# Handing score banks to the last output products in the order in which they fall free

## The chip, the cores and the metric

The kernel runs on one core of a Trainium2 chip. The metric is the device time of one execution in microseconds (us). A profile adds the span from the first to the last instruction, about 2 us shorter than that time. Engines: TensorE (matmuls; the profile calls it PE, and PEld for the loading of weights), ScalarE (ACT), VectorE (DVE), GpSimd (POOL) and SyncE (SP), which issues the stores here. L879 means line 879 of the kernel.

## The reference, cut to what matters

```python
# x: 1 x 2048 x 640;  32 heads of 20
xn = layernorm(x)
q, k, v = split(xn @ wqkv)
p = softmax(q @ k.T / sqrt(20))               # 32 x 2048 x 2048 probabilities
s = merge_heads(p @ v) @ wo                   # the "output product"
g = silu(mixer_mlp(layernorm(xn)))
return x + s * g
```

The 134 million exponentials of the softmax are the bulk. The last four blocks of 128 tokens (12 to 15) can only be finished once the last head group of their queries is done, so they form the tail of the program.

## The kernel before

The program is written by a list scheduler on the host. Every piece of work is a task; for each engine the scheduler keeps an assumed time, takes the work that is ready first by its own cost constants, and among what is ready the lowest priority number. The result is one fixed sequence of instructions for each engine, with semaphore waits where data or a PSUM bank demands one. The assumed costs decide the order only.

```python
def dv(n, rate=1.04):                 # assumed VectorE cost, ns
    return 75.0 + n * rate
...
def pe_full(fn, reads, writes, name, n):          # a full-width matmul of n columns
    t0 = max(pr.T["pe"], pr.ready("pe", reads, writes))
    c = max(pr.gate.stream(t0, n), 58.0) + pe_switch("full")    # n / 2.4 + 3 ns when warm
    pr.pe(fn, reads=reads, writes=writes, name=name, cost=c)
```

PSUM has eight banks. Bank 6 collects the attention product, banks 0 to 3 take scores for ScalarE in pairs, 4 and 5 scores for VectorE, and 7 serves all other products one at a time. When no scores are left, the score banks fall free and can hold parts of the last output products. An output product of a block is 640 columns wide: a wide part of 512 and a narrow part of 128. Each part is five "open" matmuls (L879), which need only earlier head groups, and one "closing" matmul (L884) with the last group's values in `stage_sb`.

```python
BA, BB = (5, 7), (4, 0)               # banks of blocks 14 and 15: wide, narrow
...
for i, b in enumerate(LBS):           # LBS = [14, 15]
    rq = oTall[NTB - 1] + ("wo", f"a2_{b}")
    add_job(f"tpa{i}", ...op_mms(b, ps(BA[i]), 0, 512, ..., True, False)..., rq + (f"bankoff{BA[i]}",), 60.0 + i)
    add_job(f"tpb{i}", ...op_mms(b, ps(BB[i], 128), 512, 128, ..., True, False)..., rq + (f"bankoff{BB[i]}",), 60.0 + i)
    add_job(f"tfin{i}", ...tail_fin(i)..., (f"tpa{i}", f"tpb{i}", "epL1", ...), 10.0 + i)
...
if nxt[0] >= NU:                      # no scores left to issue
    for b in act_banks:               # 0, 1, 2, 3
        if b not in bank_off and not any(b in x[1] for x in pexp):
            bank_off.add(b)
            done.add(f"bankoff{b}")
    if not bankq and 7 not in busybanks and 7 not in bank_off:
        bank_off.add(7)
        done.add("bankoff7")
```

Blocks 12 and 13 use bank 7 for their wide parts one after the other, then for both narrow parts together, which VectorE reads at L907. Only after that is bank 7 free for block 15.

Of the kernel before, what the change touches and what calls it, by code (L numbers as in the profile page):

```python
# [7 lines left out]
ALU = mybir.AluOpType  # L8
AF = mybir.ActivationFunctionType
# [273 lines left out]
class _Kern:  # L283
# [118 lines left out]
    def schedule(self):  # L402
# [22 lines left out]
        def S_(name):  # L425
            s = sl.get(name)
            if s is None:
                s = sl[name] = _Slot(name)
            return s

        bank_slot = [S_(f"bank{i}") for i in range(8)]
# [3 lines left out]
        def ps(b, n=512, off=0):  # L435
            return ps_all[:, b * 512 + off:b * 512 + off + n]

        done = set()
# [3 lines left out]
        def dv(n, rate=1.04):  # L442
            return 75.0 + n * rate

        def ac(n):
            return 90.0 + n * 0.833 + 60.0
# [340 lines left out]
        def ztmp(i, n=1):  # L787
            return zt_sb[:, 0, i % 4:i % 4 + n, :].rearrange("p a b -> p (a b)")
# [83 lines left out]
        def op_mms(b, ap, c0, n, bslot, first=True, last=True):  # L872

            steps = []
            tail = b // 4 == NTB - 1
            if first:
                for c in range(5):
                    k = 48 if c == 4 and tail else 128
                    steps.append(("pe", lambda e, c=c, k=k: e.matmul(  # L879
                        ap, oT_sb[0:k, c, b * 128:(b + 1) * 128], wo_sb[0:k, c, c0:c0 + n], start=(c == 0),  # L880
                        stop=(c == 4 and not tail)), [S_(f"oT{c}_{b // 4}"), S_("wo")], [bslot],
                        f"op{b}" if c < 4 or tail else f"opl{b}", n))
            if last and tail:
                steps.append(("pe", lambda e: e.matmul(  # L884
                    ap, stage_sb[:, (b % 4) * 128:(b % 4 + 1) * 128], wo7_sb[:, c0:c0 + n], start=False, stop=True),
                    [S_(f"stageL{last_part[b % 4]}"), S_("wo7")], [bslot], f"opl{b}", n))
            return steps
# [51 lines left out]
        def add_job(name, make, requires=(), prio=50.0):  # L939
            jobs.append(_Job(name, make if callable(make) else (lambda bk, m=make: m), requires, False, prio))  # L940
# [366 lines left out]
        for gi, (b0, nb) in enumerate(self.LN_GROUPS):  # L1307
            add_job(f"stat{gi}", stat_steps(gi), () if gi == 0 else (f"ln_s{gi - 1}",), 20.8 + b0 / 4)
            rq = (f"ln_s{gi}",) + (() if b0 < 12 else tuple(f"xT0_{d}" for d in XT[0]))
# [56 lines left out]
        for G in range(1, NG):  # L1366
            c0, c1 = 80 * (G - 1), 80 * G - 1
            for w in (1, 0):
                rq = tuple(f"qkc{w}_{j}_{tb}" for j in range(c0 // 112, c1 // 112 + 1) for tb in range(NTB)) + ("qpad",)
# [7 lines left out]
        for j in range(FC):  # L1377
            rq = hreq + xtall + ("bias", f"w1_{j // 2}")
            if j >= 4:
                rq = rq + (f"a1_{j - 4}",)  # L1380
# [10 lines left out]
        for j in range(NB):  # L1391
            rq = m1all + (f"w2_{j // 2}",) + ((f"a2_{j - 4}",) if j >= 4 else ())
# [34 lines left out]
        for p in range(NTB - 1):  # L1427
            for b in range(4 * p, 4 * p + 4):
                rq = oTall[p] + ("wo", f"ep{pidx[NG - 1, p]}", f"a2_{b}")
# [19 lines left out]
        for i, (q0, nq) in enumerate(self.QSPLIT[:-1]):  # L1449
            b0, nb = NB - 4 + q0 // 128, nq // 128  # L1450
            rq = oTall[NTB - 1] + ("wo", f"epL{i}") + tuple(f"a2_{b}" for b in range(b0, b0 + nb))
# [3 lines left out]
            add_bank_job(f"opn{b0}", opn_steps(b0, nb), rq, 30.0, NU - UP)  # L1455
            add_job(f"stl{b0}", storel_steps(b0, nb), tuple(f"res{b}" for b in range(b0, b0 + nb)), 30.0)

        BA, BB = (5, 7), (4, 0)

        def tail_fin(i):  # L1460
            b = LBS[i]
            steps = op_mms(b, ps(BA[i]), 0, 512, bank_slot[BA[i]], False, True)
            steps += op_mms(b, ps(BB[i], 128), 512, 128, bank_slot[BB[i]], False, True)
            z = ztmp(i)
            g = regC[:, b, :]
            steps.append(("act", lambda e: e.activation(z[:, 512:640], ps(BB[i], 128), AF.Copy), [bank_slot[BB[i]]],
                          [S_(f"z{i}_1")], f"tz{b}b", ac(128)))
            if i == 0:
                steps.append(("dve", lambda e: e.tensor_tensor(g[:, 0:512], ps(BA[i]), g[:, 0:512], ALU.mult),
                              [bank_slot[BA[i]], S_(f"g{b}")], [S_(f"r{b}_0")], f"tp{b}a", dv(512)))  # L1470
                steps.append(("dve", lambda e: e.tensor_tensor(g[:, 512:640], z[:, 512:640], g[:, 512:640], ALU.mult),
                              [S_(f"z{i}_1"), S_(f"g{b}")], [S_(f"r{b}_1")], f"tp{b}b", dv(128, .52)))
            else:
                steps.append(("act", lambda e: e.activation(z[:, 0:512], ps(BA[i]), AF.Copy), [bank_slot[BA[i]]],
                              [S_(f"z{i}_0")], f"tz{b}a", ac(512)))
                steps.append(("dve", lambda e: e.tensor_tensor(g, z, g, ALU.mult), [S_(f"z{i}_0"), S_(f"z{i}_1"), S_(f"g{b}")],
                              [S_(f"r{b}_0"), S_(f"r{b}_1")], f"tp{b}", dv(640, .52)))
            steps.append(("dve", lambda e: e.tensor_tensor(g, g, regA[:, b, :], ALU.add),
                          [S_(f"r{b}_0"), S_(f"r{b}_1"), S_(f"x2_{NTB - 1}")], [S_(f"res{b}")], f"tr{b}", dv(640, .52)))
            steps.append(("dma", lambda e: e.dma_start(out[0, b * 128:(b + 1) * 128, :], g), [S_(f"res{b}")], [],  # L1480
                          f"outl{b}", 163840))
            return steps

        for i, b in enumerate(LBS):
            rq = oTall[NTB - 1] + ("wo", f"a2_{b}")
            add_job(f"tpa{i}", (lambda bk, i=i, b=b: op_mms(b, ps(BA[i]), 0, 512, bank_slot[BA[i]], True, False) + [
                ("tag", f"tpa{i}")]), rq + (f"bankoff{BA[i]}",), 60.0 + i)
            add_job(f"tpb{i}", (lambda bk, i=i, b=b: op_mms(b, ps(BB[i], 128), 512, 128, bank_slot[BB[i]], True, False) + [
                ("tag", f"tpb{i}")]), rq + (f"bankoff{BB[i]}",), 60.0 + i)
            add_job(f"tfin{i}", (lambda bk, i=i: tail_fin(i)),  # L1490
                    (f"tpa{i}", f"tpb{i}", f"epL{len(self.QSPLIT) - 1}", f"x2_{NTB - 1}"), 10.0 + i)


        act_banks = [b for g in self.ACT_GROUPS for b in g]
        dve_banks = [b for g in self.DVE_GROUPS for b in g]
# [5 lines left out]
        def withdraw(bs):  # L1501
            for b in bs:
                retired.add(b)
                if b in freebanks:
                    freebanks.remove(b)
# [203 lines left out]
        bank_off = set()  # L1709
        guard = 0  # L1710
        while True:
            guard += 1
            assert guard < 400000

            if ramp[0] and "v0_15" in done:
                ramp[0] = False
                withdraw(dve_banks)
                dveready[0] = True
            if nxt[0] >= NU:
                for b in act_banks:  # L1720
                    if b not in bank_off and not any(b in x[1] for x in pexp):
                        bank_off.add(b)
                        done.add(f"bankoff{b}")
                if not bankq and 7 not in busybanks and 7 not in bank_off:
                    bank_off.add(7)
                    done.add("bankoff7")
            for dg in self.DVE_GROUPS:
                if dgrp_state[dg] == "free" and nxt[0] + self.LAST_GUARD >= NU and dveready[0] \
                        and not any(ch[0][3] == dg for ch in dchains):
                    for b in dg:  # L1730
                        if b not in bank_off:
                            bank_off.add(b)
                            done.add(f"bankoff{b}")
            activate()
            best = None
            waiting = {}
            order = sorted(("pe", "act", "dve", "pool"), key=lambda e: pr.T[e])
            acted = False
            horizon = None
            cs_by = {}  # L1740
            for e in order:
                cs = pe_cands(pr.T[e]) if e == "pe" else eng_cands(e, pr.T[e])
                cs_by[e] = cs

            bt = None
            for e in order:
                if not cs_by[e]:
                    continue
                r = min(max(x[1], pr.T[e]) for x in cs_by[e])
                if bt is None or r < bt[0]:  # L1750
                    bt = (r, e)
            if bt is None:
                break
            r, e = bt
            if e == "dve" and nxt[0] >= NU:

                soon = [max(x[1], pr.T[e]) for x in cs_by[e] if x[0] <= 12.0]
                if soon and min(soon) <= r + 130.0:
                    r = min(soon)
            ok = [x for x in cs_by[e] if x[1] <= r + 1e-6]  # L1760
            ok.sort(key=lambda x: (x[0], x[1]))
            if pr.T[e] < r:
                pr.T[e] = r
            ok[0][2]()
# [40 lines left out]
```

## Time and profile before

866.93 us, median of 3 runs (866.84 to 868.54).

| | before |
|---|---|
| span | 865.0 us |
| ScalarE busy | 845.4 us, 98% |
| VectorE busy | 823.6 us, 95% |
| TensorE busy | 797.6 us, 92% |
| last exponential ends | 855.38 us |
| tail after it | 9.6 us |

The timeline of TensorE shows its order in the tail; the columns are start, length, engine, line, operation, output and inputs, size and count, with merged rows for runs of equal instructions.

```profile
857.67 0.87 PE L879 MATMUL ps_all<-wo_sb,xnT_sb 128*128 128x128 bf16 x7
858.47 0.45 PE L884 MATMUL ps_all<-wo_sb,stage_sb 128*128 128x512 bf16 x2
858.97 1.13 PE L879 MATMUL ps_all<-wo_sb,xnT_sb 128*128 128x512 bf16 x4
860.03 0.45 PE L884 MATMUL ps_all<-wo_sb,stage_sb 128*128 128x512 bf16 x2
```

Seven narrow open matmuls (two of block 14, five of block 15), the closing pair of block 14, the wide open ones of block 15 (four of five have a record), the closing pair of block 15. A merged row shows the shape of its first instruction only.

### The profile page before, as it was taken

What the parts mean: (1) busy time and instruction counts of PE and PEld (TensorE: products, weight loads), DVE (VectorE), ACT (ScalarE), POOL (GpSimd) and SP (SyncE); (2) the same over time, 40 slices, a digit from 0 to 9 for tenths busy, and PEclk for the clock granted to TensorE, in tenths of its full rate; (3) what the DMA queues carried; (4) which work ended last, traced back from release to release, by engine and by line L of the source; (5) the groups of instructions that cost most, each with busy time, mean ns of one, the idle gap of its engine ahead of it and who ended that gap; (6) DMA issues with size and microseconds to landing.
All of it is one profiled execution on the core that took longest, in us unless ns stands there. A gap on an engine that the chain in (4) does not pass through costs nothing.

```text
span 865.0 us, 16498 instructions
## 1 busy us (share of the span) xinstructions
PE 797.6 (92%) x5828; PEld 256.1 (30%) x5918; DVE 823.6 (95%) x2047; ACT 845.4 (98%) x925; POOL 14.0 (2%) x23
## 2 busy tenths in 40 slices
PE   8899999999999999999999999999899998998997
PEld 5422222222222223222322222222222222232233
DVE  8989999999999999999999999999999999999996
ACT  7899999999999999999999999999999999999996
POOL 3200000000000000000000000000000000000000
PEclk9999999999999999999999999999999999999999
DMA  8141010011010323010013022123312201042111
GB/s 236 48 113 30 9 35 10 16 36 31 11 55 14 77 36 88 11 55 10 16 25 78 23 51 52 25 52 71 67 30 46 47 11 11 3 102 69 41 39 41
DMA packets 123350, 39.32 MB, mean 45 GB/s; under 512 B 84312, under 2 KB 122152, under 8 KB 123272
## 3 DMA queue, kind: packets, MB, share of 16 engines
q1 hardware_dynamic: 123272, 38.27, 19.4%
q8 instruction: 50, 0.82, 0.4%
q14 instruction: 28, 0.23, 0.1%
HBM read 25.88 MB, written 9.83 MB: 41 GB/s over the span
## 4 chain that ended last, share of the span: by engine, by line
ACT 87%; PE 9%; DVE 2%; POOL 1%; issue 1%; ACTq 0%; POOLq 0%
ACT pt_sb L1137 85%; PE ps_all L1109 3%; PE ps_all L1224 1%; ACT zt_sb L843 1%; PE ps_all L755 1%; PE ps_all L879 1%; ACT zt_sb L838 1%; PE ps_all L1704 1%; DVE ew_sb L1177 0%; PE ps_all L683 0%; PE ps_all L722 0%; POOL v_sb L1298 0%; PE ps_all L703 0%; DVE dpt_sb L1183 0%; PE ps_all L658 0%
## 5 line engine op out<-in xcount | busy, mean ns | idle before, releaser
L1137 ACT ACTIVATE pt_sb<-ps_all 128x1024 bf16<-128x1024 f32 x888 | 819.9, 1147 | 3.6 <-PE ps_all L1109 3.0
L1109 PE MATMUL ps_all<-qk_sb 32*128 32x512 bf16 (+1 forms) x2112 | 367.8, 377 | 48.3 <-ACT pt_sb L1137 36.7
L1177 DVE TENSOR_SCALAR ew_sb<-ps_all 128x512 uint16<-128x512 uint16 x272 | 184.2, 684 | 20.7 <-PE ps_all L1109 19.6
L1109 PEld LDWEIGHTS ps_all<-qk_sb 32*128 32x128 bf16 x2112 | 97.1, 91 | 347.0 <-ACT pt_sb L1137 299.9
L1183 DVE SCALAR_TENSOR_TENSOR dpt_sb<-ps_all,el_sb 128x512 uint16<-128x512 f32 x272 | 182.0, 684 | 1.8
L1224 PE MATMUL ps_all<-pt_sb,v_sb 128*32 128x512 bf16 (+1 forms) x1833 | 162.6, 378 | 0.3 <-issue 0.3
L1181 DVE TENSOR_TENSOR el_sb<-ev_sb,el_sb 128x512 bf16<-128x512 bf16 x272 | 111.0, 417 | 1.1
L1182 DVE TENSOR_TENSOR el_sb<-el_sb,ew_sb 128x512 bf16<-128x512 bf16 x272 | 110.2, 417 | 0.9
L1224 PE MATMUL ps_all<-dpt_sb,v_sb 128*32 128x512 bf16 (+1 forms) x279 | 83.7, 379 | 0.0
L810 PE MATMUL ps_all<-regB,regA 128*128 128x128 bf16 (+1 forms) x371 | 75.6, 300 | 2.9 <-issue 1.1
L1178 DVE TENSOR_SCALAR ev_sb<-ew_sb 128x512 bf16<-128x512 uint16 x272 | 75.3, 285 | 2.3
L810 PE MATMUL ps_all<-regC,regA 128*128 128x128 bf16 (+1 forms) x370 | 74.2, 300 | 1.8 <-issue 1.0
L1179 DVE TENSOR_SCALAR el_sb<-ew_sb 128x512 bf16<-128x512 uint16 x272 | 75.1, 284 | 0.0
L722 PE MATMUL ps_all<-xnT_sb,wqk_sb 128*112 128x512 bf16 x200 | 68.2, 405 | 0.4 <-DVE zt_sb L816 0.4
L1224 PEld LDWEIGHTS ps_all<-pt_sb,v_sb 128*32 128x32 bf16 x1833 | 35.4, 94 | 55.6 <-issue 50.2
L1696 PE MATMUL ps_all<-wrm_sb 128*128 128x512 bf16 (+1 forms) x117 | 34.0, 376 | 3.9 <-DVE ps_all L513 2.2
L810 PEld LDWEIGHTS ps_all<-regB,regA 128*128 128x128 bf16 x384 | 25.8, 97 | 39.1 <-issue 24.0
L810 PEld LDWEIGHTS ps_all<-regC,regA 128*128 128x128 bf16 x384 | 25.0, 97 | 39.8 <-issue 28.1
L1704 PE MATMUL ps_all<-wrm_sb,v_sb 128*128 128x512 bf16 x97 | 34.0, 385 | 1.3 <-issue 0.7
L755 PE MATMUL ps_all<-wv_sb,xnT_sb 128*128 128x160 bf16 (+1 forms) x160 | 33.7, 303 | 0.4 <-DVE pk_sb L1030 0.3
L879 PE MATMUL ps_all<-wo_sb,xnT_sb 128*128 128x128 bf16 (+3 forms) x151 | 30.2, 298 | 1.1 <-issue 0.5
L722 PEld LDWEIGHTS ps_all<-xnT_sb,wqk_sb 128*112 128x112 bf16 x200 | 20.7, 127 | 30.5 <-issue 13.4
(89 smaller groups left out, 354.4 us busy)
## 6 DMA issues: line engine op xcount, KB each, us to landing
regA<-in_B_w_dram SPq DMA_DIRECT2D x6, 1024.0 KB
regA<-in_B_w_dram SPq DMA_DIRECT2D x8, 768.0 KB
qkT_scratch_dram<-pk_sb SPq DMA_DIRECT2D x40, 112.0 KB
qk_sb<-qkT_scratch_dram SPq DMA_DIRECT2D x56, 80.0 KB
regA<-in_A_x_dram SPq DMA_DIRECT2D x6, 640.0 KB
on_scratch_dram<-on_sb SPq DMA_DIRECT2D x124, 20.0 KB
out_dram<-regC SPq DMA_DIRECT2D x3, 640.0 KB
wqk_sb<-in_A_wqkv_dram SPq DMA_DIRECT2D x2, 680.0 KB
```

Of the source, the lines that this page charges most:

```text
L722: steps.append(("pe", lambda e, dc=dc: e.matmul(ps_all[0:112, bk * 512:(bk + 1) * 512], wqk_sb[:, dc * 1280 + c0:dc * 1280 + c0 + 112], xn ...
L810: steps.append(("pe", lambda e, k=k: e.matmul(ps(bk, n), wap[:, k, col0:col0 + 128], rows[:, k, c0:c0 + n], start=(k == 0), stop=(k == nk ...
L1109: pr.pe(lambda e, outp=outp, lhsT=lhsT, rhs=rhs, g=g: e.matmul(outp, lhsT, rhs, start=True, stop=True, tile_position=(32 * g, 0)), reads=q ...
L1137: tk = pr.act(lambda e: e.activation(outp, inp, AF.Exp, bias=-self.OFFS * math.log(2.0) / 128.0, scale=math.log(2.0) / 128.0), reads=[bank ...
L1177: (lambda e: e.tensor_scalar(w3, lo, 0x7FFF, None, ALU.bitwise_and), bs, [sw], dv(N)),
L1178: (lambda e: e.tensor_scalar(v_, w_, 1.0 / 256.0, -128.0, ALU.mult, ALU.add), [sw], [sv], dv(N, .26)),
L1179: (lambda e: e.tensor_scalar(l_, w_, a3 / 65536.0, (b3 - 64.0 * a3) / 256.0, ALU.mult, ALU.add), [sw], [sl_], dv(N, .26)),
L1181: (lambda e: e.tensor_tensor(l_, v_, l_, ALU.mult), [sv, sl_], [sl_], dv(N, .52)),
L1182: (lambda e: e.tensor_tensor(l_, l_, w_, ALU.mult), [sl_, sw], [sl_], dv(N, .52)),
L1183: (lambda e: e.scalar_tensor_tensor(o_, zr, -(self.OFFS - 16256.0), l_, ALU.add, ALU.add), bs + [sl_], [S_(f"dpt{s0 + i}") for i in range( ...
L1224: pr.pe(lambda e, outp=outp, lhsT=lhsT, rhs=rhs, k=k, g=g: e.matmul(outp, lhsT, rhs, start=(k == 0), stop=(k == NB - 1), tile_position=(0, ...
L1704: pe_full(lambda e: e.matmul(ps(AB), zero, wrm_sb[:, P:P + 512], start=new, stop=new), [S_("warm"), S_("v_ones")], [sl_acc], "warmz", 512)
```

## The change

The fixed list of banks goes. Every bank that falls free is appended to a list, and block 14 wide, 14 narrow, 15 wide and 15 narrow take the first four. The intent is that no product waits for a bank while another stands empty.

```diff
-        BA, BB = (5, 7), (4, 0)
+        tbank = []
...   in tail_fin and in the two open jobs, everywhere:
-  ps(BA[i]) ... bank_slot[BA[i]]            ps(BB[i], 128) ... bank_slot[BB[i]]
+  ps(tbank[2 * i]) ... bank_slot[tbank[2 * i]]   ps(tbank[2 * i + 1], 128) ... bank_slot[tbank[2 * i + 1]]
...
-  rq + (f"bankoff{BA[i]}",), 60.0 + i)      rq + (f"bankoff{BB[i]}",), 60.0 + i)
+  rq + (f"tbank{2 * i}",), 60.0 + i)        rq + (f"tbank{2 * i + 1}",), 60.0 + i)
...
+        def bank_out(b):
+            bank_off.add(b)
+            tbank.append(b)
+            done.add(f"tbank{len(tbank) - 1}")
...   where a bank falls free (three places; for 7 likewise):
-                        bank_off.add(b)
-                        done.add(f"bankoff{b}")
+                        bank_out(b)
```

More of the change, by code (lines that the diff above doesn't have):

```diff
@@ L1456, in schedule @@
             add_job(f"stl{b0}", storel_steps(b0, nb), tuple(f"res{b}" for b in range(b0, b0 + nb)), 30.0)
-        BA, BB = (5, 7), (4, 0)
+        tbank = []
         def tail_fin(i):
             b = LBS[i]
-            steps = op_mms(b, ps(BA[i]), 0, 512, bank_slot[BA[i]], False, True)
-            steps += op_mms(b, ps(BB[i], 128), 512, 128, bank_slot[BB[i]], False, True)
+            steps = op_mms(b, ps(tbank[2 * i]), 0, 512, bank_slot[tbank[2 * i]], False, True)
+            steps += op_mms(b, ps(tbank[2 * i + 1], 128), 512, 128, bank_slot[tbank[2 * i + 1]], False, True)
             z = ztmp(i)
             g = regC[:, b, :]
-            steps.append(("act", lambda e: e.activation(z[:, 512:640], ps(BB[i], 128), AF.Copy), [bank_slot[BB[i]]],
+            steps.append(("act", lambda e: e.activation(z[:, 512:640], ps(tbank[2 * i + 1], 128), AF.Copy), [bank_slot[tbank[2 * i + 1]]],
                           [S_(f"z{i}_1")], f"tz{b}b", ac(128)))
             if i == 0:
-                steps.append(("dve", lambda e: e.tensor_tensor(g[:, 0:512], ps(BA[i]), g[:, 0:512], ALU.mult),
-                              [bank_slot[BA[i]], S_(f"g{b}")], [S_(f"r{b}_0")], f"tp{b}a", dv(512)))
+                steps.append(("dve", lambda e: e.tensor_tensor(g[:, 0:512], ps(tbank[2 * i]), g[:, 0:512], ALU.mult),
+                              [bank_slot[tbank[2 * i]], S_(f"g{b}")], [S_(f"r{b}_0")], f"tp{b}a", dv(512)))
                 steps.append(("dve", lambda e: e.tensor_tensor(g[:, 512:640], z[:, 512:640], g[:, 512:640], ALU.mult),
@@ L1473, in tail_fin @@
             else:
-                steps.append(("act", lambda e: e.activation(z[:, 0:512], ps(BA[i]), AF.Copy), [bank_slot[BA[i]]],
+                steps.append(("act", lambda e: e.activation(z[:, 0:512], ps(tbank[2 * i]), AF.Copy), [bank_slot[tbank[2 * i]]],
                               [S_(f"z{i}_0")], f"tz{b}a", ac(512)))
@@ L1485, in schedule @@
             rq = oTall[NTB - 1] + ("wo", f"a2_{b}")
-            add_job(f"tpa{i}", (lambda bk, i=i, b=b: op_mms(b, ps(BA[i]), 0, 512, bank_slot[BA[i]], True, False) + [
-                ("tag", f"tpa{i}")]), rq + (f"bankoff{BA[i]}",), 60.0 + i)
-            add_job(f"tpb{i}", (lambda bk, i=i, b=b: op_mms(b, ps(BB[i], 128), 512, 128, bank_slot[BB[i]], True, False) + [
-                ("tag", f"tpb{i}")]), rq + (f"bankoff{BB[i]}",), 60.0 + i)
+            add_job(f"tpa{i}", (lambda bk, i=i, b=b: op_mms(b, ps(tbank[2 * i]), 0, 512, bank_slot[tbank[2 * i]], True, False) + [
+                ("tag", f"tpa{i}")]), rq + (f"tbank{2 * i}",), 60.0 + i)
+            add_job(f"tpb{i}", (lambda bk, i=i, b=b: op_mms(b, ps(tbank[2 * i + 1], 128), 512, 128, bank_slot[tbank[2 * i + 1]], True, False) + [
+                ("tag", f"tpb{i}")]), rq + (f"tbank{2 * i + 1}",), 60.0 + i)
             add_job(f"tfin{i}", (lambda bk, i=i: tail_fin(i)),
                     (f"tpa{i}", f"tpb{i}", f"epL{len(self.QSPLIT) - 1}", f"x2_{NTB - 1}"), 10.0 + i)
+        def bank_out(b):
+            bank_off.add(b)
+            tbank.append(b)
+            done.add(f"tbank{len(tbank) - 1}")
         act_banks = [b for g in self.ACT_GROUPS for b in g]
@@ L1721, in schedule @@
                     if b not in bank_off and not any(b in x[1] for x in pexp):
-                        bank_off.add(b)
-                        done.add(f"bankoff{b}")
+                        bank_out(b)
                 if not bankq and 7 not in busybanks and 7 not in bank_off:
-                    bank_off.add(7)
-                    done.add("bankoff7")
+                    bank_out(7)
             for dg in self.DVE_GROUPS:
@@ L1731, in schedule @@
                         if b not in bank_off:
-                            bank_off.add(b)
-                            done.add(f"bankoff{b}")
+                            bank_out(b)
             activate()
```

## The prediction

> **What bounds the kernel now.** I read the page's totals first, then the chain of work that ended last over the whole span, then the same chain and the timeline for the last 11 us, because the change touches nothing else.
>
> ```profile
> PE 797.6 (92%) x5828; PEld 256.1 (30%) x5918; DVE 823.6 (95%) x2047; ACT 845.4 (98%) x925; POOL 14.0 (2%) x23
> ...
> ACT 87%; PE 9%; DVE 2%; POOL 1%; issue 1%; ACTq 0%; POOLq 0%
> ```
>
> ScalarE is busy 98% of 865.0 us: the 888 exponentials of the scores are the kernel, and nothing in the diff touches one of them. What the change can move is what comes after the last exponential. The timeline of ScalarE from 845 us shows where that is: 12 exponentials from 844.02 for 11.36 us, so the last ends at 855.38, then nothing for 3.58 us until the small copy at 858.95. The tail is therefore 865.0 - 855.4 = 9.6 us, and the chain in it (start, length, what) is:
>
> ```profile
> 855.61 0.54 PE ps_all L879 x2
> 856.14 0.33 PE ps_all L1224 x8
> 856.48 0.66 PE ps_all L879 x8
> 857.13 0.16 PE ps_all L884
> 857.29 0.38 PE ps_all L879 x5
> 857.67 0.16 PE ps_all L884
> 857.84 0.70 PE ps_all L879 x7
> 858.54 0.38 PE ps_all L884 x2
> 858.92 0.05 issue
> 858.97 1.13 PE ps_all L879 x4
> 860.10 0.39 PE ps_all L884 x2
> 860.49 0.02 issue
> 860.51 0.28 ACT zt_sb L1466
> 860.79 0.50 ACTq L253
> 861.29 0.02 issue
> 861.31 0.50 DVE regC L1476
> 861.81 0.02 issue
> 861.84 0.49 DVE regC L1478
> ```
>
> The reader is to see that TensorE is itself the chain from 855.6 to 860.5, with 0.05 us of waiting in it. L1224 is the last attention product; L879 the part of an output product that needs no last head group; L884 its closing matmul, which needs `stage_sb`. In program order the pieces after the last attention product are: 3 of block 14's narrow product (128 columns), the narrow products of blocks 12 and 13 (6 + 6), 2 more of block 14, 5 of block 15's narrow product, block 14's two closing matmuls (858.47), 5 of block 15's wide product (512 columns), block 15's two closing matmuls (860.03). Then ScalarE copies, VectorE multiplies and adds, and the store is issued at 862.36; the span ends 2.6 us later.
>
> **What the change does to the bank order.** A bank "falls free" in the host program's list when the group using it has its last exponential behind it. I followed the bookkeeping of the kernel before for its order: 5, then 4 (VectorE's), then 0 and 1 together (the exponential of units 2044 and 2045), then 2 and 3, last 7, which holds the narrow products of blocks 12 and 13 until VectorE has read it. The fixed list gives block 14 banks 5 and 4, block 15 wide bank 7 and narrow bank 0. By order of freedom block 14 gets 5 and 4 again, and block 15 wide gets 0 and narrow gets 1. So the whole change is this: block 15's five open wide matmuls no longer depend on bank 7, that is, on VectorE's product at L907.
>
> ```profile
> 857.61 0.45 DVE L1266 STREAM_TRANSPOSE stage_sb<-on_sb 128x256 bf16<-128x256 bf16 x1
> 857.98 0.39 DVE L907 TENSOR_TENSOR regC<-ps_all,regC 128x256 bf16<-128x256 f32 x1
> 858.40 0.49 DVE L919 TENSOR_TENSOR regC<-regC,regA 128x640 bf16<-128x640 bf16 x1
> 858.90 0.69 DVE L1469 TENSOR_TENSOR regC<-ps_all,regC 128x512 bf16<-128x512 f32 x1
> ```
>
> L907 ended at 858.37. TensorE came to block 15's wide product only after block 14's closing pair, whose second matmul started at 858.70. So the dependence that is removed was met 0.3 us before TensorE could have used it. That is the main reading: **the wait removed is worth nothing by itself**.
>
> **What it reorders.** The list is a greedy one: TensorE takes whatever is ready, by priority, and the closing matmuls of block 14 (priority 10) beat the open ones of block 15 (61) once `stage_sb` is ready. Before the point where block 15's first matmul is issued nothing changes: its narrow product was already eligible, at the same priority and from the same exponential, and was never picked earlier; the wide one cannot be either. From there the program's own constants decide (they are bookkeeping, taken for the order alone; no time below comes from them). With X the end of the last attention product, it supposes 58 ns per narrow matmul plus one switch of 110, so 17 narrow ones end at X + 1096; a wide one 512/2.4 + 3 = 216; and `stage_sb` ready at X + 1790. In the kernel before, five narrow ones ended at X + 1386 and the list believed that TensorE then idled 404 ns. Now both products are ready with equal priority, and the wide job stands first in the list. It starts wide ones at X + 1096, 1312, 1529 and 1745; the last is just short of 1790. So I expect four wide ones, block 14's closing pair, the fifth wide, five narrow, block 15's closing pair.
>
> On the chip the supposed idle 404 ns do not exist. From 856.41 to 858.47 TensorE ran 22 narrow matmuls (20 open, 2 closing), 2.06/22 = 94 ns each instead of 58, and `stage_sb` was ready at 858.06 while TensorE was still busy to 858.47.
>
> **What the Trainium skill says.** "TensorE: Matmul & The Clock Gate", section "Back-to-back issue gap", gives about 81 ns per matmul at N=128 in a real stream, and says that the isolated formula undercounts there (56 ns). This trace agrees roughly: 94 ns with the 48-row ones among them. For N=512 it gives 131 ns sustained and 216 isolated; this trace does not show 131: the wide starts at 858.97 and 859.19 are about 0.21 apart. "PSUM — Partial Sum Buffer", section "Engine vs sequencer instructions", says that matmuls start and complete in program order. So a ready closing matmul cannot overtake the open ones placed ahead of it. The trace agrees: block 14's pair, ready at 858.06, started at 858.47, after everything placed ahead of it.
>
> **The sum.**
> - Removed: one dependence already met; 0.0 us.
> - TensorE's work between 856.41 and block 15's closing pair is the same set of matmuls in another order. The 48-row matmuls at the end of each five cost about 0.1 us more than the others (859.40 to 859.71 is 0.31 where neighbours are 0.21), and their number and isolation do not change. The closing pair therefore stays at 860.03, within 0.1.
> - Block 14's closing pair: block 14's last open matmul started at 857.82, the next at 857.98. Four wide ones from 857.98 at 0.213 put it at 857.98 + 0.85 = 858.83 instead of 858.47: 0.36 us later.
> - VectorE after it: the product at L1469 moves from 858.90 to about 859.26. What follows it up to the last add of block 13 (860.17 + 0.48 = 860.65) ends at about 861.01. The last block's product was to start at 861.31. It has 0.66 us of slack, so 0.36 is swallowed; VectorE's idle 0.66 us there shrinks to 0.3.
> - ScalarE's copies and the last two VectorE instructions: unchanged lengths (0.28, 0.59, 0.49, 0.49).
> - Stores: the first two, issued at 860.28 and 860.68, move about 0.36 later. Their data kept the DMA engines busy from about 861.0 to 862.5, the last store's from about 863.0 to 864.0 (stretches of half a microsecond). The gap of about 0.5 us swallows 0.36, perhaps with 0.1 left over.
> Sum: 0.0, between -0.1 and +0.2 us of 866.9.
>
> **The rivals.** (a) The gain the list hopes for: it fills 404 supposed idle ns, so the end comes 0.4 us sooner, 866.5. For it: an order that starts the wide product earlier looks better on paper. Against it: the chain shows 0.05 us of waiting on TensorE in that stretch; there is no hole to fill. (b) A new wait: block 14's closing pair later by more than 0.66 us, should the list put all ten open matmuls of block 15 ahead (the five narrow ones are ahead already, the five wide ones add 5 x 0.213 = 1.07); then VectorE carries the end and it is 0.4 later, plus the store's share, 867.4. Against it: the priority of the closing pair stops the list after four. (c) The list shifts everywhere and the exponentials' cadence changes by a per cent (8 us): nothing for it, since free banks are handed out only in the last 10 units. (d) A large gain, if bank 7 truly held TensorE: it would need TensorE idle from 858.4 on, and it was not; even all 1.1 us of the five wide matmuls is 0.13%.
>
> **Range and chances.** Every rival lies within 1.2 us of 866.9, under 0.15%; 2% is 17 us. The range is set by the spread of executions (866.84 to 868.54 before) rather than by the change: 866.2 to 867.9. Within 2%: 0.994; the rest is split for what I may have misread.
>
> **What would show it.** Right: five L879 wide matmuls on the chain before block 14's L884 pair or around it; that pair near 858.8; the last L884 pair near 860.0; VectorE's wait before L1476 down from 0.66 to about 0.3; the last store near 862.4; the span 865.0 within 0.3. Wrong: the last L884 pair at 859.7 or sooner (rival a: TensorE had a hole); VectorE with no wait before L1476 and that line later than 861.4 (rival b); a shift of ScalarE's last exponential from 855.4 (rival c).

## The result, and the profile after

The changed kernel: 866.88 us, median of 6 runs (866.44 to 867.05); before, in the same rounds and those above, 867.07 us (866.84 to 868.54, 6 runs). The ratio is 0.9995, 95% interval 0.9982 to 1.0007: the same. A ratio here is the mean time of one kernel's fast runs over that of the other's of the same rounds, so not quite the ratio of the medians. The span of the profiled run is 864.8 us.

A comparison of the two programs' sequences shows the same order on ScalarE, VectorE, GpSimd and SyncE. TensorE's differs only in its last 14 tasks of 5918: before, five narrow of block 15, the closing pair of 14, five wide of 15, the closing pair of 15; now four wide of 15, the pair of 14, one wide, five narrow, the pair of 15. The chain of work that ended last, from the last open matmuls of block 14 on:

```profile
857.65 1.18 PE ps_all L879 x6
858.84 0.23 PE ps_all L884
859.07 0.02 issue
859.09 0.40 DVE regC L1470
859.49 0.21 issue
859.70 0.23 DVE regC L1472
859.92 0.15 issue
860.07 0.23 PE ps_all L884
860.31 0.02 issue
860.33 0.28 ACT zt_sb L1467
```

And TensorE's and VectorE's timelines of the same stretch:

```profile
857.49 1.35 PE L879 MATMUL ps_all<-wo_sb,xnT_sb 128*128 128x128 bf16 x6
858.67 0.43 PE L884 MATMUL ps_all<-wo_sb,stage_sb 128*128 128x512 bf16 x2
859.04 0.87 PE L879 MATMUL ps_all<-wo_sb,xnT_sb 48*128 48x512 bf16 x6
860.07 0.22 PE L884 MATMUL ps_all<-wo_sb,stage_sb 128*128 128x128 bf16 x1 [0.16 <-DVE regC L1472]
...
859.09 0.69 DVE L1470 TENSOR_TENSOR regC<-ps_all,regC 128x512 bf16<-128x512 f32 x1 [0.38 <-PE ps_all L884]
860.36 0.48 DVE L919 TENSOR_TENSOR regC<-regC,regA 128x640 bf16<-128x640 bf16 x1
861.13 0.49 DVE L1477 TENSOR_TENSOR regC<-zt_sb,regC 128x640 bf16<-128x640 bf16 x1 [0.29 <-ACT zt_sb L1475]
```

All of the tail must be read from a common point, because the tails of two executions start at different times: the last attention product (L1224) started at 856.07 before and at 855.89 after, on identical programs up to there. From that start to the end of the span it is 8.91 us in both (with the traces' unrounded spans, 864.985 and 864.800 us; 8.93 and 8.91 with the rounded ones). Block 14's closing pair starts 2.40 us after it before, 2.78 now. VectorE waits 0.38 us for it before L1470 and only 0.29 instead of 0.66 before L1477.

One trap is in these lines. The chain now seems to run through VectorE, and TensorE's last row to wait for L1472. It is not so: the wide closing matmul of block 15, which stands between 859.04's row and 860.07, has no record (some matmul records are missing from a trace), and the profile filled the hole with the instruction that happened to end there. The next section has an execution of the same order with that record (860.45, two matmuls).

### The profile page after: what moved, and what is told of

It reads as the page before. It is cut to its first block, busy times and chain, and to the rows that moved or that the text cites. A ratio compares the mean times of both kernels' runs of the same rounds, so it can differ in the third digit from the quotient of the medians.

```text
span 864.8 us, 16498 instructions
## 1 busy us (share of the span) xinstructions
PE 798.6 (92%) x5828; PEld 257.1 (30%) x5918; DVE 823.5 (95%) x2047; ACT 845.3 (98%) x925; POOL 14.0 (2%) x23
## 4 chain that ended last, share of the span: by engine, by line
ACT 87%; PE 10%; DVE 2%; issue 1%; ACTq 0%
ACT pt_sb L1137 85%; PE ps_all L1109 3%; PE ps_all L1224 1%; ACT zt_sb L843 1%; PE ps_all L755 1%; PE ps_all L1702 1%; PE ps_all L879 1%; ACT zt_sb L838 1%; DVE ew_sb L1177 0%; PE ps_all L683 0%; PE ps_all L1710 0%; PE ps_all L722 0%; PE ps_all L703 0%; DVE dpt_sb L1183 0%; DVE el_sb L1181 0%
## 5 line engine op out<-in xcount | busy, mean ns | idle before, releaser
L1224 PE MATMUL ps_all<-pt_sb,v_sb 128*32 128x512 bf16 (+1 forms) x1833 | 162.7, 378 | 0.3 <-issue 0.3
L1224 PE MATMUL ps_all<-dpt_sb,v_sb 128*32 128x512 bf16 (+1 forms) x279 | 83.7, 379 | 0.0
L1224 PEld LDWEIGHTS ps_all<-pt_sb,v_sb 128*32 128x32 bf16 x1833 | 35.4, 94 | 55.5 <-issue 50.4
```

What stands on the lines that cost most here:

```text
L1224: pr.pe(lambda e, outp=outp, lhsT=lhsT, rhs=rhs, k=k, g=g: e.matmul(outp, lhsT, rhs, start=(k == 0), stop=(k == NB - 1), tile_position=(0, ...
```

## The experiments

The device times scatter by half a microsecond and more, and the scatter goes with the granted clock over the run: among the eleven runs of before beside e1 to e4, those at 0.999 and above took 866.45 to 867.20 us, those at 0.995 to 0.997 took 868.8 to 870.05. (A mean of 0.998 alone says little: it counts a drop after TensorE's last matmul too. e1's profiled run has 0.998, and its clock fell at 862.2 us, when the last matmul had ended at 860.6.) So each verdict rests on two things: the time, and the tail's length, measured from the start of VectorE's first transpose after the last attention product (856.53 before) to the end of the span (unrounded, from the packed traces). It is 8.46 us before and after.

| run | median us (runs) | before in the same rounds | ratio, 95% interval | tail us |
|---|---|---|---|---|
| e1 the change again | 867.58 (5) | 867.11 | 1.0000, 0.9987 to 1.0013 | 8.45 |
| e2 banks alone | 867.03 (5) | 867.11 | 0.9997, 0.9984 to 1.0010 | 8.45 |
| e3 closing pair last | 867.65 (6) | 867.11 | 1.0006, 0.9991 to 1.0022 | 8.55 |
| e4 ten matmuls fewer | 867.26 (6) | 867.11 | 0.9997, 0.9982 to 1.0012 | 7.81 |
| e5 bank 7 late, before | 868.07 (5) | 866.89 | 1.0012, 1.0000 to 1.0024 | 9.39 |
| e6 bank 7 late, after | 867.76 (5) | 866.89 | 1.0012, 1.0000 to 1.0024 | 8.95 |

e1 to e4 ran on one chip in the same rounds, e5 and e6 with e7 and e8.

**e1, the change again.** No edit.

> The changed kernel again, for the size of what is to be told apart. Theory (the removed dependence was met already, TensorE never idles in the last 5 us before its end, the later closing pair of block 14 is swallowed by VectorE's slack): within 0.3 us of before. The list's own bookkeeping, which believes that 0.47 us is saved: 0.4 to 0.5 us faster, ratio 0.9995.

The tail is 8.45 us and the time not told from before's. The gain of 0.47 us that the list believed in is not in the trace; an interval of 0.13% (1.1 us) either way could not have excluded it alone.

**e2, the banks alone.** The new banks, but the wide product of block 15 must wait for the closing pair of block 14, so TensorE keeps the order of before.

```diff
+            steps.append(("tag", f"tclose{i}"))          # after the two closing matmuls in tail_fin
...
-  rq + (f"tbank{2 * i}",), 60.0 + i)
+  rq + (f"tbank{2 * i}",) + (("tclose0",) if i else ()), 60.0 + i)
```

> The new banks, but block 15's wide product held back until block 14's closing pair is issued, so that TensorE's order is that of before. Theory: no dependence mattered, so within 0.3 us of before, block 14's closing pair again 2.4 us after the start of the last attention product, TensorE's last pair 3.96 us after it. Rival (the freed bank gives some 0.4 us and the later closing pair takes it back): 0.3 to 0.4 us faster than both.

TensorE's timeline:

```profile
858.59 0.45 PE L884 MATMUL ps_all<-wo_sb,stage_sb 128*128 128x512 bf16 x2
859.09 1.13 PE L879 MATMUL ps_all<-wo_sb,xnT_sb 128*128 128x512 bf16 x4
860.15 0.45 PE L884 MATMUL ps_all<-wo_sb,stage_sb 128*128 128x512 bf16 x2
```

The last attention product started at 856.19, so the pairs come 2.40 and 3.96 us after it, exactly as in before (858.47 and 860.03 less 856.07). With another bank and nothing else changed, nothing moved by more than 0.01 us. So no gain by the bank hides behind a loss by the order.

**e3, the closing pair last.** Its priority is put behind the open matmuls.

```diff
-                    (f"tpa{i}", f"tpb{i}", f"epL{len(self.QSPLIT) - 1}", f"x2_{NTB - 1}"), 10.0 + i)
+                    (f"tpa{i}", f"tpb{i}", f"epL{len(self.QSPLIT) - 1}", f"x2_{NTB - 1}"), 70.0 + i)
```

> The changed kernel with block 14's closing pair put behind all ten open matmuls of block 15. Theory: TensorE's last pair stays 3.96 us after the start of the last attention product, block 14's pair comes about 3.7 us after it instead of 2.4, VectorE's slack of 0.66 us is used up and the end comes about 0.2 us later than in before (0.1 to 0.4). Rival (a later closing pair costs what it is late): 1.0 to 1.3 us later.

VectorE's timeline:

```profile
859.99 0.69 DVE L1470 TENSOR_TENSOR regC<-ps_all,regC 128x512 bf16<-128x512 f32 x1 [0.89 <-remote]
861.26 0.48 DVE L1477 TENSOR_TENSOR regC<-zt_sb,regC 128x640 bf16<-128x640 bf16 x1
```

Block 14's product (L1470) is 0.91 us later after the transpose than in the changed kernel (859.99 less 856.33 is 3.66; 859.09 less 856.34 is 2.75), and the idle time before L1477 is gone. The tail grew by 0.10 us against before: the low end of what was expected. VectorE's slack alone did not swallow the lateness. ("Remote" is the missing record again: the wide closing matmul that L1470 waits for has none here.) One other thing moved too: the list put the add of block 13 ahead of block 14's product on VectorE, into time in which VectorE now waited, and its store ahead. Such an add takes 0.41 us of VectorE here (860.85 to 861.26); an estimate from that is that without the move the end would have come about 0.5 us later than in before. So a good part of the small loss is that luck of the list, which the expectation had not foreseen.

**e4, ten matmuls fewer.** A wrong result: of the twelve narrow matmuls of blocks 12 and 13 only the two closing ones stay.

```diff
-                    steps += op_mms(b0 + i, ps(bk, 128, 128 * i), 512, 128, bank_slot[bk])
+                    steps.append(("pe", ...one closing matmul, start=True, stop=True...))   # blocks 12, 13
...   and the adds res12, res13: priority 30.0 -> 9.0
```

> Wrong result on purpose: ten open narrow matmuls of blocks 12 and 13 left out after the last attention product (and the adds of those blocks put ahead of block 14's on VectorE). Theory (TensorE's work bounds this stretch): its last pair comes 0.9 to 1.1 us sooner, VectorE or the copies bind then, the end comes 0.4 to 0.7 us sooner. Rival (VectorE's chain or the stores set the end already): within 0.2 us of before.

TensorE's last rows:

```profile
858.89 0.43 PE L884 MATMUL ps_all<-wo_sb,stage_sb 128*128 128x512 bf16 x2
859.26 0.23 PE L879 MATMUL ps_all<-wo_sb,xnT_sb 48*128 48x128 bf16 x1
859.42 0.45 PE L884 MATMUL ps_all<-wo_sb,stage_sb 128*128 128x512 bf16 x2
```

The transpose started at 856.89, so the last pair comes 2.53 us after it instead of 3.50 (860.03 less 856.53): 0.97 us sooner. The ten matmuls took 0.96 us in before: two stretches of 0.48, from 856.58 to 857.06 and from 857.13 to 857.61. The last block's product on VectorE starts 0.97 us sooner as well (860.70 less 856.89 is 3.81; 861.31 less 856.53 is 4.78). The tail fell by only 0.65 us, because the list here put block 14's add between the last two VectorE instructions. So the amount of TensorE's work sets this stretch. The device time does not show it (866.13 to 868.19 us in six runs). In the profiled execution the tail began 0.36 us later, so the span is only 0.3 us shorter than before's; and the time is 2.55 us above the span there (1.93 to 2.57 in the six runs), against 1.90 to 1.95 in the runs of before in the same rounds. Why is not known.

**e5 and e6, bank 7 later.** The removed dependence, made to matter. Three VectorE products without use are put ahead of the one that empties bank 7, with cost 0 in the list, so that no order changes; once in the kernel before, once in the changed one.

```diff
+                if b0 == NB - 4:
+                    for _ in range(3):
+                        steps.append(("dve", lambda e: e.tensor_tensor(el_sb[:, 0, :], el_sb[:, 0, :], el_sb[:, 0, :], ALU.mult),
+                                      [bank_slot[bk], S_("el0")], [S_("el0")], "fill", 0.0))
```

> The kernel before with three idle VectorE products (0.42 us each) put ahead of the one that empties bank 7, with no cost in the list, so the order stays. Theory: bank 7 then falls free 1.25 us later, 0.9 us after TensorE wants it; block 15's wide product waits, and the end comes 0.8 to 1.0 us later. Rival (bank 7 doesn't gate the wide product at all): as the changed kernel with the same delay.

> The changed kernel with the same three products in the same place. Theory: TensorE does not wait for it (last pair 3.96 us after the start of the last attention product), only VectorE's own chain gets later by 1.25 us less the 0.38 us that it idled before block 14's product, less the 0.3 us before block 15's: 0.5 to 0.6 us later than before, 0.3 to 0.4 us less than in the other run of this pair. Rival: both the same.

The kernel before, with the delay (TensorE, then VectorE):

```profile
859.54 1.35 PE L879 MATMUL ps_all<-wo_sb,xnT_sb 128*128 128x512 bf16 x5 [0.75 <-DVE regC L911]
860.83 0.45 PE L884 MATMUL ps_all<-wo_sb,stage_sb 128*128 128x512 bf16 x2
...
859.07 0.42 DVE L911 TENSOR_TENSOR regC<-ps_all,regC 128x256 bf16<-128x256 f32 x1
```

The changed one, with the delay:

```profile
859.64 0.88 PE L879 MATMUL ps_all<-wo_sb,xnT_sb 48*128 48x512 bf16 x6
860.45 0.45 PE L884 MATMUL ps_all<-wo_sb,stage_sb 128*128 128x512 bf16 x2
```

In the kernel before TensorE now waits 0.75 us for L911, the product that empties bank 7, and its last pair comes 4.43 us after the transpose (860.83 less 856.40). In the changed kernel it comes 3.51 us after it (860.45 less 856.94), where it always was. The tails are 0.93 and 0.49 us longer than before's; the second is VectorE's own chain and a little under the 0.5 to 0.6 expected. So the change does remove a dependence, worth 0.44 us in the tail when bank 7 is 1.25 us late; the times, 868.07 and 867.76, point the same way but are not told apart. In the profiled execution of the kernel before, bank 7 was not late.

**e7 to e11, a kernel to beat both.** If TensorE's work bounds the tail, open matmuls should leave it. Up to about 846 us TensorE runs filler matmuls (L1696), which compute nothing and are meant to keep its clock up, in bank 7. e7 and e8 run block 12's five wide open matmuls there, and hold the bank until the closing one; e9 and e10 also add zero-weight fillers into the held bank; e11 is e10 again.

```diff
-                add_bank_job(f"op{b}_0", op_steps(b), rq, 30.0, NU - UP)                  # for block 12:
+                add_bank_job("op12_open", open_steps(12), ...without epL0..., 30.0, 2018)  # e8, e9: 2012; e10, e11: 2016
+                add_job("op12_close", close_steps(12), ("op12_open", "epL0"), 30.0)
...   e9 to e11:
+            e.matmul(ps(wb, n), zero, wrm_sb[:, P:P + n], start=False, stop=False)         # zero weights, held bank
```

> A kernel to beat both: block 12's wide product split, its five open matmuls issued from unit 2018 on in place of filler matmuls that only keep the clock up, its bank held until the closing matmul. Theory: TensorE has some 1.1 us less to do in its last saturated stretch, its last pair and the end come 0.4 to 1.0 us sooner than in before. Rival (ScalarE's exponentials or the chain behind the last attention product set the end): within 0.2 us.

> The same from unit 2012 on: more fillers gone, and the list puts only nine open matmuls behind the last attention product. Theory: 0.6 to 1.2 us sooner than before if the granted clock stays at 1.0; the list itself fears a cold clock near 843 us, and if that comes the exponentials wait and it is 1 us or more later.

> Block 12's open wide product early as in the two runs before, from unit 2012 on, but with filler matmuls against zero weights added into its held bank, so that the clock stays up. Theory: the granted clock stays at 1.0 to the end in every run, TensorE has some 1.1 us less to do in its last saturated stretch, and the time is 0.2 to 0.8 us below before, with no run above 869. Rival (the fillers' lack was not the cause of the cold clock in the earlier pair): runs at 870 and above again.

> The same from unit 2016 on, which leaves two zero fillers instead of six. Theory: as the other of this pair if two suffice; where the clock drops in some runs, those are 5 us and more longer and the others 0.2 to 0.8 us below before.

> The last kernel again, for a second sample and a profile of a usual run. If its gain is real: four runs in five or more at 866.1 to 866.6, the end 8.0 to 8.2 us after the start of the last attention product (8.93 in before), the granted clock 1.0 up to the last exponential. If the first sample was luck: its median within 0.2 us of before's.

e7: four runs at 866.50 to 866.91 us and two at 873.31 and 874.82 (before in the same rounds: 866.36 to 868.08). e8: all five at 868.78 to 871.54. The profiled execution of e7 is one of the long ones. Its stretches from 846 us (busy time and count of PE, PEld, DVE, ACT and POOL, then the granted clock, the DMA share and GB/s):

```profile
846.00:850.00 4.00, 3.21 (x49) 1.43 (x37) 4.00 (x13) 4.00 (x5) 0.00 (x0) 1.00 0.00 0
850.00:854.00 4.00, 3.81 (x34) 1.24 (x33) 2.15 (x5) 3.42 (x4) 0.00 (x0) 0.55 0.02 4
854.00:858.00 4.00, 4.00 (x28) 1.04 (x28) 2.35 (x5) 2.52 (x3) 0.00 (x0) 0.50 0.00 0
```

The granted clock halves at about 850 us and ScalarE, fed late, falls from 4.00 to 2.52 us busy in four. The Trainium skill describes this: "TensorE: Matmul & The Clock Gate", section "What's actually happening", has the clock halved after an idle window of about 3.4 us that does not start with the kernel. The 0.50 agrees. The idle window does not: in the 3.41 us before the drop, from 847.01 to 850.42, TensorE was busy for 2.86 us, and its longest wait there was 0.42 us. That the same program keeps its clock in four runs of six and loses it in two would fit a window whose place differs from run to run; no run here shows it. This profile has an earlier drop as well, from 727.5 to 731.0 us, far ahead of the moved matmuls.

e9's fillers did not secure the clock: its three runs at 0.999 and above took 867.06 to 867.86 us, and three more at 0.994, 0.988 and 0.984 took 871.81, 874.37 and 877.84. The expectation failed. Whether six fillers are too few, or the clock was lost in another stretch, is open, as none of the long runs was profiled. The profile shows another fault, and e8's too: the list issues the matmul before its transposed input has landed, and the scores behind it in TensorE's order wait as well. e8's TensorE:

```profile
842.75 0.39 PE L879 MATMUL ps_all<-wo_sb,xnT_sb 48*128 48x512 bf16 x1 [1.03 <-DMA xnT_sb<-on_scratch_dram]
```

e10 and e11, four units later, have no such wait in e11's profile, and both have a median of 866.46 us against 866.92 and 867.04. e11's tail, from the last attention product at 856.46 to the end, is 8.10 us instead of 8.91. But 5 of their 10 runs were below 0.999 (three of them at 867.65 to 868.54 us), against 2 of 20 of before in the same rounds. That the edit costs this clock is not shown. The profiled execution of e10 is the one at 868.54 us, and it lost its clock at 727.9 us, for 3.4 us, more than 100 us ahead of the first moved matmul; e11 at 866.46 us kept it there (the columns are those of e7's stretches):

```profile
727.00:732.00 5.00, 4.47 (x16) 1.27 (x15) 5.00 (x15) 4.63 (x5) 0.00 (x0) 0.66 0.23 16
727.00:732.00 5.00, 4.95 (x30) 1.52 (x32) 4.87 (x14) 5.00 (x6) 0.00 (x0) 1.00 0.23 16
```

The first line is e10's. Its last exponential ends 2.08 us after e11's (857.82 against 855.74), and the tails are equal, 8.10 us. The five at 0.999 and above took 866.12 to 866.49 us, mean 866.29, where the 18 of before took 866.30 to 867.39, mean 866.94; over all runs the ratios are 0.9991 (0.9978 to 1.0004) and 1.0001 (0.9988 to 1.0015). The way to a shorter tail is shown, 0.81 us in both profiles, and the chosen runs are 0.65 us faster; but a kernel that beats the one before over all its runs is not.

## Why the prediction was right

- **No value in the removed wait.** Right, by e2. e5 measures the slack as well: VectorE's product that empties bank 7 ended 1.25 us later after the transpose than before (859.49 less 856.40 is 3.09; 858.37 less 856.53 is 1.84) and TensorE's first wide matmul was held to 859.54. In before that one has no record; 0.21 us before 858.97 it is at 858.76, 2.23 us after the transpose, against 3.14 here. So of 1.25 us late, 0.91 was felt and 0.34 was slack: the prediction said 0.3.
- **The new order.** Right to the matmul: four wide, the pair, one wide, five narrow, the pair.
- **TensorE's work conserved, its last pair at the same distance.** Right: 3.96 us after the last attention product in before and in e2; in the new order the narrow half of the pair starts 4.18 us after it (860.07 less 855.89), where e2's, 0.23 us behind its wide half, starts at 4.19. e4 shows the converse: take ten matmuls away and the pair comes 0.97 us sooner.
- **Block 14's pair 0.36 us later.** It measured 0.38 (2.78 less 2.40).
- **Swallowed by VectorE's 0.66 us, with 0.3 left.** It measured 0.29. e3 spends all of it and loses 0.10 us, with the help of the add that moved.
- **The stores 0.36 us later, hidden.** The first was issued 4.58 us after the last attention product (860.47 less 855.89) instead of 4.21, the last one at the same 6.29 and 6.28; the tail did not grow.
- **One reading was wrong, without harm to the sum.** The prediction has narrow matmuls at 94 ns each instead of the list's 58, and finds the 81 ns of the page that it cites roughly confirmed. 94 is only a mean. In the single starts of before's trace, narrow matmuls over full 128 rows follow each other after 56 ns (856.47, 856.53, 856.58), as the list believes. The one over 48 rows starts 152 ns after its neighbour (856.75, 856.90), and the next one 158 ns after it (857.06): about 0.2 us more than two full ones. Four of the 22 are such, 0.8 of the 2.06 us. So it is these that fill the hole which the list believed in, and no term of the list stands for them. That TensorE had no hole was read from measured starts, and stands.
- **The sum, 0.0 between -0.1 and +0.2.** The tail changed by less than 0.01 us, the median by -0.19, which is within the scatter of the runs.

Of the rivals, (a), the 404 ns hole of the list, fell: its belief rests on 58 ns for every narrow matmul, and on nothing more for those over 48 rows. (b) was tried by e3 in a stronger form. There block 14's product on VectorE came 1.29 us later after the transpose than in before (3.66 against 858.90 less 856.53, 2.37), and the end 0.10 us later rather than the 0.4 estimated. By the estimate at e3, the add that moved ahead makes most of that difference: (b)'s sum was sound, and only its premise, ten open matmuls ahead of the pair, did not come about. (c) and (d) did not occur.

## What to carry to other kernels

Removing a wait pays only if the waiting engine would have had nothing else to do: ask in the trace when the dependence was met and when the engine came to it, not whether the wait exists. If an engine is busy through a stretch, reordering its work moves the intermediate results about, and the end only if the total falls. A list scheduler's gain is worth what its constants are worth: 58 ns is right for a full narrow matmul (56 measured), but about 0.2 us for each one over 48 rows was missing, and that made a hole of 0.4 us out of a full engine. Here lies the untried step: from 856.41 to block 15's closing pair there are five of them, about 1 us by this figure. Whether 128 rows padded with zeros, or 48-row matmuls side by side, would save it, no run tested.

## What the Trainium skill lacked or had wrong

- "TensorE: Matmul & The Clock Gate", section "Back-to-back issue gap": neither of its sustained figures appeared. Full wide matmuls start 0.216 us apart (858.97, 859.18, 859.40) and not 131 ns, full narrow ones 56 ns apart (856.47, 856.53) and not 81: both stand where its isolated formula puts them, 216 and about 56 ns.
- The same section has nothing on a matmul over fewer rows among full ones: one over 48 rows, and the one after it, each start about 0.1 us later than a neighbour would (wide starts at 859.40, 859.71 and 860.03 in before, where neighbours are 0.216 apart; narrow ones 0.152 and 0.158 us apart, where neighbours are 0.056).
- "TensorE: Matmul & The Clock Gate", section "What's actually happening": it does not say how busy TensorE has to be within a window, and its "idle window" does not fit e7: the clock halved after 3.41 us in which TensorE was busy for 2.86. The same program kept its clock in four runs (0.999 to 1.0, 866.50 to 866.91 us) and lost it in two (0.990 and 0.987, 873.31 and 874.82 us).
- No page says how far such drops spread the times of a kernel that is tuned around them: for the kernel before, 866.45 to 867.20 us at a mean granted clock of 0.999 and above and up to 870.05 at 0.995. One drop of 3.4 us, at 728 us in e10's profile, goes with a last exponential 2.08 us later than in e11's, of the same program.
